# Local-window attention with an FFN: the values of a pair of heads as one TensorE block, and the order drawn up anew

## The chip, the cores and the metric

One core of a Trainium2 chip. The metric is the device time of one execution in microseconds (us). Engines: TensorE (PE) for matmuls, with its weight loads (PEld) beside them; VectorE (DVE); ScalarE (ACT); GpSimd (POOL); SyncE (SP), which issues the DMAs.

## The reference, cut to what is computed

```python
# q_l,k_l,v_l: (8, 8, 512, 64); q_g,k_g,v_g: (8, 8, 32, 64)
k_all, v_all = concat([k_g, k_l], 2), concat([v_g, v_l], 2)
out_g = softmax(q_g @ k_all.T / 8) @ v_all                  # 32 global rows see everything
s_ll  = where(abs(i - j) <= 32, q_l @ k_l.T / 8, -1e9)      # local rows: a window, and the global keys
out_l = softmax(concat([q_l @ k_g.T / 8, s_ll])) @ concat([v_g, v_l])
x = concat([out_g, out_l], 2) -> (8 * 544, 512)             # 8 heads x 64
h = x @ w_in                                                # 512 -> 2048, weights in float64
return (h * erf(softplus(h))) @ w_out                       # 2048 -> 512
```

## The kernel before

**The work.** There are 64 heads (8 batches of 8). `attention(b, h, key)` records the steps of one head. For a pair of heads one TensorE block of 64x32 tiles makes the scores of both (tiles `s`, 32 blocks). For each head DVE adds the mask and takes the maximum, ACT takes the exponentials (tile `sm`; for the first `BIASED` heads with the maximum as a bias, after them with a subtraction on DVE or POOL), PE transposes them in full 128x128 shape (`t`), ACT or DVE copies the result to SBUF (`pt`, two buffers), and PE makes the values `o` in 128x32 tiles: a block of 16 small products for each head, 64 blocks in all. DVE normalizes them into `xn`. For every four heads `attention_global(b, j, ...)` does the same for the 32 global rows: scores `ga`, `gb` (64x32 tiles), transposes `gt`, values `go` (128x32 tiles), 16 blocks of each.

The FFN runs as full 128x128 products of 512 columns, a high and a low part of each factor (three matmuls for one product): `h` (`unit`), the gate (`gate`: softplus and erf on ACT, tiles `sp`, `gh`, `gl`), `op` (`project`). A first pass takes three eighths of the hidden columns, batch by batch, between the attention heads; a second pass takes the rest when attention is done, with the products `pa` to `pd` of a seven-product scheme for pairs of batches. Weights come as float64 and are turned into float32 parts on DVE and ACT (`to_fp32`, `keep_in`, `keep_unit`; tiles `top_in`, `top_out`, `top_l_in`, `top_k_out`).

**What sets the order.** Nothing runs when `attention` or `gate` is called: each step is recorded by `Program.add(ways, key, fn, reads, writes, ...)`, where `ways` names the engines that may do it with an assumed time for each, and `key` is its due time. `Program.schedule()` (line 159) plays the steps through once, on the host, with these times. For each engine it takes the ready step of lowest key whose buffers are free and writes the order out; that order, engine by engine, is the program's. `crowded` (line 190) keeps the number of PE instructions within a stretch of time under a limit (`CROWD`, `STRETCH`, `EVADE`); `PORT` charges DVE for working beside POOL; `SHARED` (line 40) names the range of keys in which a step may go to POOL as well as DVE; `fill` puts spare matmuls into PE's idle time at the start. Keys come from the constants at the top (`HKEYS` for the heads, `GOFF`, `POFF`, `GATE1`, `PROJ1` and others for the FFN). PSUM has two banks with tag `h` and six with tag `a`; scores, transposes, values and `op` share the six.

Of the kernel before, what the change touches and what calls it, by code (L numbers as in the profile page):

```python
# [21 lines left out]
P = 128  # L22
# [7 lines left out]
CROWD, STRETCH, EVADE = 254, 4.013, 0.27  # L30
# [3 lines left out]
HKEYS = ((0, -5.063), (10, -3.503), (22, 0.608), (64, 30.894))  # L34
STEP, GKEY = 0.023, -0.868
QLEAD, VLEAD, RLEAD, XLEAD = 0.459, 0.046, 0.011, 2.412
# [4 lines left out]
TPAIR = 2.626  # L41
KEEP, KSTEP, FIRST = 16.147, 2.595, (-2.849, 0.951)
CVO = (50.84, 53.645, 53.996, 48.864, 55.397)
QLEAD2, XDEL, SLOTS = 10.999, 1.259, 11
GATE1, GATE2, PROJ1, PROJ2 = (3.909, 9.618, 11.922), (13.773, 23.579, 27.539), 17.617, 26.859
SPT = 0.35
BIAS, AHEAD = 1.072, 15.956
# [3 lines left out]
SLACK, PORT = {"PE": 0.8, "SP": 0.8}, 0.7  # L51
# [7 lines left out]
WLEAD = 0.011  # L59
LATER, GFIRST = 8, (-2.568, -2.486)  # L60
NORMAL = 1.125 * 2.0**-15
STRAIGHT, XLATE = True, -0.932
# [44 lines left out]
class Program:  # L107
# [9 lines left out]
    def add(self, ways, key, fn, reads=(), writes=(), moved=0.0, heat=0, ins=None):  # L117
# [9 lines left out]
        op.heat, op.ins = heat, ins or heat // 256  # L127
# [24 lines left out]
        self.ops.append(op)  # L152
        return op
# [5 lines left out]
    def schedule(self):  # L159
# [28 lines left out]
        warmth, issued = [], []  # L188

        def crowded(n):  # L190

            t = 0.0
            for at, m in reversed(issued):
                n += m
                if at <= now - STRETCH:
                    break
                if n > CROWD:
                    t = max(t, at + STRETCH - now)
                    break
            return t  # L200

        def fill():
            dur = fill_dur if now > COLD else 2 * fill_dur
            until["PE"] = max(since, now) + dur
            heapq.heappush(events, (until["PE"], -1, 0, None))
            if now >= since:
                op = Op()
                op.eng, op.ways, op.fn, op.key, op.start, op.heat = "PE", {"PE": dur}, fill_fn, 0.0, now, fill_heat
                op.new, op.bufs = [], []
                order.append(op)  # L210
                warmth.append((now, fill_heat))

# [6 lines left out]
        while events or any(o.eng is None for o in self.ops) and ahead < 1e3:  # L219
# [14 lines left out]
            while picked:  # L234
                picked = False
                for e, q in ready.items():
# [4 lines left out]
                    while until[e] <= now and (dense or q and q[0][0] <= line[front].key + ahead):  # L241
# [4 lines left out]
                        item = dense.pop(0) if dense_only and dense else heapq.heappop(q)  # L246
# [6 lines left out]
                        if any(free[k] < n for k, n in need.items()) or elsewhere(op, e):  # L253
                            skipped.append(item)
                            continue
# [50 lines left out]
def kernel(  # L306
# [109 lines left out]
    def attention(b, h, key):  # L416
# [17 lines left out]
        if h % 2 == 0:  # L434
# [39 lines left out]
        if biased:  # L474
            add({"ACT": 1.05}, key, exps, [TAB, MX], [SM])
# [16 lines left out]
        PT = abuf([P, 4, P], f"pt_{nm}", "pt", 2)  # L492
        add({"PE": 0.5}, key + STEP * 2, transposes, [SM, CS], [T, PT], heat=512, ins=8)
# [3 lines left out]
        def values():  # L497
# [9 lines left out]

        add({"PE": 0.64}, key + STEP * 3, values, [PT, VA, VB], [O], heat=1040, ins=64)
        RS = abuf([P, 4, 1], f"rs_{nm}", "rs", 2)
        add({"DVE": 0.07},  # L510
            key + STEP * 3,
            lambda: dve.tensor_scalar(RS.ap, O.ap[:, :, D : D + 1], 1e-9, None, op0=ALU.add),
            [O],
            [RS],
        )
        add({"DVE": 0.09}, key + STEP * 3, lambda: dve.reciprocal(RS.ap, RS.ap), [], [RS])

        def norm(e):
            if e == "DVE":
                dve.tensor_tensor(  # L520
                    XN.ap[:, :, r0 : r0 + D], O.ap[:, :, :D], RS.ap.to_broadcast([P, 4, D]), ALU.mult
                )
            else:
                for t in range(4):
                    act(XN.ap[:, t, r0 : r0 + D], O.ap[:, t, :D], AF.Copy, scale=RS.ap[:, t, :])

        add({"DVE": 0.34, "ACT": 0.85}, key + STEP * 3, norm, [O, RS], [XN])
# [20 lines left out]
        if h % 4 == 3:  # L548
            more = b, h // 4, [st["va", i] for i in range(4)], [st["qk", i] for i in range(2)]
            if b == 0 and LATER:  # L550
                held.append((*more, GFIRST[h // 4]))
            else:
                attention_global(*more, key + GKEY)
# [4 lines left out]
    held, GTURN, X0 = [], fixed(None), {}  # L558
# [33 lines left out]
    def attention_global(b, j, VA, qk, key):  # L592
        nm = f"{b}_{j}"
# [19 lines left out]
        add({"PE": 1.15}, key, scores, [*qk[0], *qk[1]], [GA, GB, GTURN], heat=1088, ins=32)  # L613
        M, NM = abuf([P, 2], f"gm_{nm}", "gm", 2), abuf([P, 1], f"gn_{nm}", "gn", 2)
        add({"DVE": 0.57}, key, lambda: dve.tensor_reduce(M.ap[:, 0:1], GA.ap, axis=AX.X, op=ALU.max), [GA], [M])
# [44 lines left out]
        add({"PE": 0.88}, key + STEP * 3, values, [GT, *VA], [O], heat=1560, ins=96)  # L660
# [44 lines left out]
    def to_fp32(key, src, name, TOP, ABS, deps, lead=RLEAD):  # L705
# [21 lines left out]
        add({"DVE": 1.75}, key, bits, [RAW], [TOP.buf])  # L727
# [12 lines left out]
    class View:  # L740
# [3 lines left out]
        def ap(self):  # L744
            return self.f(self.buf.ap)
# [58 lines left out]
    def keep_in(q, key):  # L804
# [9 lines left out]
        def part_of(m, a, k):  # L814
            A, ap = a
            O = mbuf([P, 2, 2, P], F32R, f"part_{q}_{m}", "os", 4)
            add({"ACT": 0.36, "DVE": 0.25}, k, lambda e: copy(e, O.ap[:, 0], ap()), [A.buf], [O])
            add(
                {"POOL": 0.88, "DVE": 0.4},
# [14 lines left out]
        def sum_of(out, a, b, op, k):  # L834
            add(
                {"DVE": 0.4, "POOL": 0.8},
# [19 lines left out]
    def load_x(ps, c, key):  # L856
# [5 lines left out]
        for i in range(2):  # L862
# [23 lines left out]
            add({"DVE": 0.0014 * n, "ACT": 0.0022 * n + 0.1}, k, split_hi, [RAW], [HI])  # L886
            add({"POOL": 0.0048 * n + 0.3, "DVE": 0.0026 * n + 0.15}, k, split_lo, [RAW, HI], [LO])
# [39 lines left out]
    def gate(ps, c, us, key, after=(), turn=(), line=()):  # L927
# [3 lines left out]
        def erf():  # L931
# [10 lines left out]
            {"ACT": 2.57 + 1.29 * (ps == 0) + 1.09 * len(us)},  # L942
# [6 lines left out]
        for n, ((v, Hb, more), SPb) in enumerate(zip(us, SP)):  # L949
# [5 lines left out]
                {"DVE": 0.75, "POOL": 1.5},  # L955
# [5 lines left out]
            add({"DVE": 0.43, "ACT": 0.55}, k, lambda e, SPb=SPb, GH=GH: copy(e, GH.ap, SPb.ap), [SPb, *after], [GH, *turn])  # L961
            add(
                {"DVE": 0.75, "POOL": 1.5},
# [16 lines left out]
    def project(ps, c, G, at, order, after=None):  # L980
# [15 lines left out]
        for t in range(nt):  # L996
            for n, rows in enumerate(order):
                need = [x for g, _, v in rows for x in (*G[g], *W["out", ps, v // 2])]
                add(
                    {"PE": 0.685 * len(rows)},  # L1000
# [82 lines left out]
    def pair_blocks(pr, key):  # L1083
# [11 lines left out]
        def block(name, n, A, k):  # L1095
# [17 lines left out]
            add({"DVE": 0.95, "ACT": 1.1}, k, hi, [A, ATTN], [HI])  # L1113
            add({"POOL": 2.8, "DVE": 1.55}, k, lo, [A, HI, ATTN], [LO])
            blocks[name] = (HI, LO)

        def sum_of(out, a, b, op, k):
            add(
                {"DVE": 1.2, "POOL": 2.5},
# [20 lines left out]
    def products(name, q, X, key):  # L1140
# [17 lines left out]
        def product(n, m, x, start, k):  # L1158
            add({"PE": 1.37}, k, lambda: mm(n, m, x, start), [M[m], *X[x]], [bank[n]], heat=3072)
# [63 lines left out]
    def last_unit(q, X, key):  # L1223
# [17 lines left out]
        for r in range(2):  # L1241
            add({"PE": 1.43}, key + 0.01 * r, lambda r=r: mm(r), [*M.values(), *(t for b in X.values() for t in b)], [HP], heat=3072)
# [127 lines left out]
```

## Time and profile before

| | |
|---|---|
| time of the runs | 920.95 us median of 3 (920.82 to 922.83) |
| the profiled execution's span | 920.8 us, 22337 instructions |
| busy: PE, PEld | 897.3 us (97%), 720.7 us (78%) |
| busy: DVE, ACT, POOL | 667.2 us (72%), 570.1 us (62%), 61.7 us (7%) |
| chain of work that ended last | PE 84%, DMA 6%, DVE 6%, issue 2%, ACT 1% |
| DMA over the span | 188.23 MB, mean 204 GB/s |

An engine's busy time is the union of its instructions. Matmuls are pipelined, so their listed durations overlap; what one costs is read from the distance of starts. A number in brackets behind a row is the idle time of the engine just before it, with what ended it; "issue" means that the engine waited for nothing that the profile shows.

### The profile page before, as it was taken

How to read it: one execution, taken by the hardware profiler on the slowest of the kernel's cores; microseconds unless marked ns; L12 is line 12 of the kernel's file. 1: busy time of each engine (PE TensorE's matmuls, PEld its weight loads, DVE VectorE, ACT ScalarE, POOL GpSimd, SP SyncE). 2: the span in 40 equal slices, each digit the busy share in tenths (PEclk: the TensorE clock that was granted, in tenths of full speed). 3: DMA queues.
4: the chain of work that ended last, by engine and by line, in shares of the span. 5: the costliest groups of instructions: out<-in, count | busy, mean ns of one | idle time of the engine just before them, and what ended most of it. 6: DMA issues, size and time to landing. Idle time of an engine off the chain costs nothing.

```text
span 920.8 us, 22337 instructions
## 1 busy us (share of the span) xinstructions
PE 897.3 (97%) x8814; PEld 720.7 (78%) x8814; DVE 667.2 (72%) x1733; ACT 570.1 (62%) x975; POOL 61.7 (7%) x51
## 2 busy tenths in 40 slices
PE   8799989999999999999999999999999999999998
PEld 5576767777777778888888888888888888888886
DVE  4698989978979897768857867648674677445562
ACT  4578986656757676866855569425862476335760
POOL 0003543131100000000000000000000000000000
PEclk9899999999999999999999999999999999999999
DMA  9698986979697885823458953644355535455121
GB/s 338 224 305 265 317 270 214 301 240 285 213 313 252 274 281 177 293 110 124 151 204 299 343 181 124 217 139 154 89 183 173 193 91 159 126 170 167 66 80 68
DMA packets 110017, 188.23 MB, mean 204 GB/s; under 512 B 15576, under 2 KB 39384, under 8 KB 109912
## 3 DMA queue, kind: packets, MB, share of 16 engines
q1 hardware_dynamic: 109912, 186.79, 61.8%
q8 instruction: 70, 1.15, 0.5%
q14 instruction: 35, 0.29, 0.1%
HBM read 145.59 MB, written 41.16 MB: 203 GB/s over the span
## 4 chain that ended last, share of the span: by engine, by line
PE 84%; DMA 6%; DVE 6%; issue 2%; ACT 1%; SPq 1%; DVEq 0%; ACTq 0%
PE op L344 38%; PE h L344 12%; PE pd L344 6%; PE pc L344 6%; PE pa L344 6%; PE pb L344 3%; PE o L344 3%; PE t L345 3%; PE s L344 2%; DMA wq<-part 2%; PE h_g L344 2%; DMA vb<-in_vB_dram 1%; DMA xsc<-xT 1%; DMA k<-in_kE_dram 1%; PE gt L345 1%
## 5 line engine op out<-in xcount | busy, mean ns | idle before, releaser
L344 PE MATMUL op<-wouth,gh 128*128 128x512 f32 x544 | 215.9, 397 | 0.4 <-DVE mx L356 0.4
L344 PE MATMUL op<-wouth,gl 128*128 128x512 f32 x544 | 212.1, 390 | 0.2 <-issue 0.2
L344 PE MATMUL op<-woutl,gh 128*128 128x512 f32 x544 | 212.0, 390 | 0.0
L347 ACT ACT_TABLE_LOAD x108 | 138.6, 1283 | 2.7 <-PEq L1357 0.7
L344 PEld LDWEIGHTS op<-wouth,gh 128*128 128x128 f32 x544 | 102.2, 188 | 23.2 <-issue 2.0
L344 PEld LDWEIGHTS op<-wouth,gl 128*128 128x128 f32 x544 | 102.1, 188 | 21.8
L344 PEld LDWEIGHTS op<-woutl,gh 128*128 128x128 f32 x544 | 102.2, 188 | 19.6
L356 DVE TENSOR_TENSOR gl<-sp,gh 128x512 fp32r<-128x512 f32 x129 | 89.4, 707 | 27.8 <-ACT gh L346 18.3
L346 ACT ACTIVATE gh<-sp 128x512 fp32r<-128x512 f32 x94 | 57.2, 627 | 83.8 <-PE op L344 71.1
L344 PE MATMUL h<-xh,winh 128*128 128x512 f32 (+1 forms) x216 | 85.8, 397 | 0.3 <-ACT hs L346 0.3
L344 PE MATMUL h<-xh,winl 128*128 128x512 f32 (+1 forms) x216 | 82.5, 382 | 0.0
L344 PE MATMUL h<-xl,winh 128*128 128x512 f32 (+1 forms) x216 | 82.5, 382 | 0.0
L346 ACT ACTIVATE sp<-sp 128x512 f32<-128x512 f32 x136 | 75.9, 621 | 0.5
L356 DVE CUSTOM_DVE_ANT_0 sm<-s,cs 128x128 f32<-128x128 f32 x256 | 57.1, 283 | 12.2 <-DMA cs<-in_cst_dram 7.0
L344 PE MATMUL pa<-xh_B,wq 128*128 128x512 f32 x160 | 55.8, 389 | 0.0
L344 PE MATMUL pd<-xh_T,wq 128*128 128x512 f32 x160 | 55.6, 389 | 0.0
L346 ACT ACTIVATE hs<-h 128x512 f32<-128x512 f32 x44 | 26.0, 595 | 41.5 <-PE h L344 41.3
L344 PEld LDWEIGHTS h<-xh,winh 128*128 128x128 f32 x216 | 41.1, 190 | 9.3 <-issue 1.0
L356 DVE TENSOR_TENSOR pair<-u,pc 128x512 f32<-128x512 f32 x40 | 27.4, 684 | 27.6 <-PE pc L344 27.5
L344 PEld LDWEIGHTS h<-xh,winl 128*128 128x128 f32 x216 | 41.0, 190 | 8.0
L344 PEld LDWEIGHTS o<-va,pt 128*32 128x32 f32 x768 | 31.7, 109 | 19.1 <-issue 11.2
L344 PEld LDWEIGHTS h<-xl,winh 128*128 128x128 f32 x216 | 41.1, 190 | 6.7
(163 smaller groups left out, 1687.0 us busy)
## 6 DMA issues: line engine op xcount, KB each, us to landing
wq<-wq SPq DMA_DIRECT2D x140, 256.0 KB, 3.3
vb<-in_vB_dram SPq DMA_DIRECT2D x64, 325.0 KB, 5.2
rx<-xsc SPq DMA_DIRECT2D x30, 512.0 KB, 5.4
va<-in_vA_dram SPq DMA_DIRECT2D x64, 195.0 KB, 4.8
k<-in_kE_dram SPq DMA_DIRECT2D x32, 384.0 KB, 5.1
wq<-part SPq DMA_DIRECT2D x35, 256.0 KB, 4.3
q<-in_qT_dram SPq DMA_DIRECT2D x32, 272.0 KB, 4.9
part<-os SPq DMA_DIRECT2D x34, 256.0 KB, 3.4
```

Source lines behind the costliest of these rows:

```text
L344: pe = lambda n, *a, **k: pinned(nc.tensor.matmul(n, *a, **k))
L345: tr = lambda *a, **k: pinned(nc.tensor.transpose(*a, **k))
L346: act = lambda *a, **k: pinned(nc.scalar.activation(*a, **k))
L347: table = lambda name: pinned(nc.scalar.preload_act_table_set(name))
L356: return lambda *a, **k: pinned(f(*a, **k))
```

## The change

It does five things.

1. From head 16 on (`PAIRED`), the values of the two heads of a pair are one recorded step (`pair`), which waits for the `pt` of both heads. Their normalizations (`normalize`, the same operations as before) follow it. In batches 6 and 7 the values of the global rows are in the same step as the pair of heads 2, 3 or 6, 7 (`GOJOIN`), and the global scores in the same step as that pair's scores (`GSJOIN`, `joint`).
2. The planner gives each PE step a mode (`S` for scores, `O` for values, `F` for full products and transposes) and adds a time from `TURN` where the mode changes. While PE is in mode S or O, a ready step of the same mode counts as `NEAR` = 10.893 keys earlier.
3. `PORT` goes from 0.7 to 1.0, with the charge limited to 1.6 us in place of 1.5 times the step's own time; many assumed times are reset. `SHARED` ends at key 0.191 instead of 17.961, so that steps with later keys go to DVE alone.
4. `pt` and `sm` have four buffers each instead of two. `crowded` uses a longer stretch (5.5) between 8 and 36 us, and `EVADE` goes from 0.27 to 0.515.
5. All keys are drawn up anew, and `BIASED` is 28 instead of 30.

```diff
-CROWD, STRETCH, EVADE = 254, 4.013, 0.27
+CROWD, STRETCH, EVADE = 254, 4.013, 0.515
+LOADED = (8.0, 36.0, 5.5)
-HKEYS = ((0, -5.063), (10, -3.503), (22, 0.608), (64, 30.894))
+HKEYS = ((0, -4.186), (11, -1.133), (22, 2.638), (64, 28.435))
-GOFF, POFF = 1.452, 1.865
-WIN, WOUT = (-2.963, -1.41, -1.202), (3.958, 3.604, 3.417)
-BIASED, AG = 30, 3
-SHARED = (-99.0, 17.961)
+GOFF, POFF = 6.702, 2.351
+WIN, WOUT = (-1.182, -0.883, -2.317), (6.11, 7.043, 6.921)
+BIASED, AG = 28, 3
+SHARED = (-99.0, 0.191)
-KEEP, KSTEP, FIRST = 16.147, 2.595, (-2.849, 0.951)
+KEEP, KSTEP, FIRST = 17.877, 2.241, (18.664, 20.991)
-GATE1, GATE2, PROJ1, PROJ2 = (3.909, 9.618, 11.922), (13.773, 23.579, 27.539), 17.617, 26.859
+GATE1, GATE2, PROJ1, PROJ2 = (20.257, 19.313, 15.951), (15.777, 23.93, 18.604), 21.217, 28.842
-SLACK, PORT = {"PE": 0.8, "SP": 0.8}, 0.7
+SLACK, PORT = {"PE": 0.8, "SP": 0.8}, 1.0
+TURN = {"FS": 0.11, "FO": 0.11, "SF": 0.35, "OF": 0.28, "SO": 0.31, "OS": 0.30}
+NEAR = 10.893
+PAIRED, GOJOIN, GSJOIN, PTS = 16, 6, 6, 4
+SMS, SPARED = 4, 0
-LATER, GFIRST = 8, (-2.568, -2.486)
+LATER, GFIRST = 9, (-3.478, -13.073)
...
+            stretch = LOADED[2] if LOADED[0] <= now < LOADED[1] else STRETCH
...
-                        item = dense.pop(0) if dense_only and dense else heapq.heappop(q)
+                        if dense_only and dense:
+                            item = dense.pop(0)
+                        elif e == "PE" and mode != "F" and NEAR:
+                            item = min(q, key=lambda i: (i[0] - (NEAR if i[2].mode == mode else 0.0), i[1]))
+                            q.remove(item)
+                            heapq.heapify(q)
+                        else:
+                            item = heapq.heappop(q)
...
+                        if e == "PE":
+                            dur += TURN.get(mode + op.mode, 0.0)
+                            mode = op.mode
                         if e == "DVE" and op.port:
-                            dur += PORT * min(max(0.0, until["POOL"] - now), 1.5 * dur)
+                            dur += PORT * min(max(0.0, until["POOL"] - now), 1.6)
...
-            add({"PE": 1.24}, key, scores, [Q, K], SS, heat=2048, ins=128)
+            if h % 4 == 2 and b >= GSJOIN:
+                GA, GB, more = global_scores(b, h // 4, [st["qk", 0], (Q, K)])
+                G0[b, h // 4] = GA, GB
+
+                def joint():
+                    scores()
+                    more()
+
+                add({"PE": 1.9}, key, joint, [*st["qk", 0], Q, K], [*SS, GA, GB, GTURN], heat=3136, ins=160, mode="S")
+            else:
+                add({"PE": 1.02}, key, scores, [Q, K], SS, heat=2048, ins=128, mode="S")
...
-        SM = abuf([P, 4, P], f"sm_{nm}", "s", 2)
+        SM = abuf([P, 4, P], f"sm_{nm}", "s", SMS)
...
-        PT = abuf([P, 4, P], f"pt_{nm}", "pt", 2)
+        PT = abuf([P, 4, P], f"pt_{nm}", "pt", PTS)
...
-        add({"PE": 0.64}, key + STEP * 3, values, [PT, VA, VB], [O], heat=1040, ins=64)
+        if h % 4 == 3 and b >= GOJOIN:
+            joined = global_probs(*group, key + GKEY)
+        if NH * b + h - h % 2 < PAIRED:
+            add({"PE": 0.55}, key + STEP * 3, values, [PT, VA, VB], [O], heat=1040, ins=64, mode="O")
+            normalize(O, XN, r0, nm, key)
+        elif h % 2 == 0:
+            st["o"] = values, [PT, VA, VB], O, r0, nm
+        else:
+            first, need, O0, *rest = st["o"]
+            last, more, GO = joined or (None, [], None)
+
+            def pair():
+                first()
+                values()
+                if last:
+                    last()
+
+            add({"PE": 1.11 + 0.72 * (GO is not None)},
+                key + STEP * 3,
+                pair,
+                [*need, PT, VA, VB, *more],
+                [O0, O] + [GO] * (GO is not None),
+                heat=2080,
+                ins=128 + 96 * (GO is not None),
+                mode="O",
+            )
+            normalize(O0, XN, *rest, key)
+            normalize(O, XN, r0, nm, key)
+            if joined:
+                global_rows(*group[:2], GO, key + GKEY)
```

`global_scores`, `global_probs` and `global_rows` are the three parts of `attention_global`, their operations unchanged.

## Rows read from the trace of the kernel before

**Rows 1.** Stages: us; busy PE, PEld, DVE, ACT, POOL (instructions); clock; DMA; GB/s.

```profile
58.00:160.00 102.00, 93.65 (x1780) 71.35 (x1781) 93.93 (x332) 85.65 (x185) 39.54 (x29) 0.98 0.83 268
160.00:364.00 204.00, 201.01 (x3329) 155.15 (x3328) 179.09 (x631) 132.35 (x237) 18.68 (x15) 1.00 0.82 263
364.00:920.80 556.80, 553.26 (x2531) 461.62 (x2529) 356.74 (x594) 319.79 (x470) 0.00 (x0) 1.00 0.49 162
```

**Rows 2.** Timeline of PE: start, us, instruction; one head's values among full products.

```profile
207.47 0.39 PE L344 MATMUL h<-xh,winl 128*128 128x512 f32 x1
207.79 0.24 PE L344 MATMUL o<-va,pt 128*32 128x65 f32 x1
...
208.38 0.55 PE L345 MATMUL gt<-cs,pg 128*128 128x128 f32 x3
```

**Rows 3.** Timeline of PE: values of two heads side by side.

```profile
215.42 0.24 PE L344 MATMUL o<-va,pt 128*32 128x65 f32 x1
...
216.47 0.50 PE L344 MATMUL h<-xh,winh 128*128 128x512 f32 x1
216.81 0.39 PE L344 MATMUL h<-xl,winh 128*128 128x512 f32 x1
```

**Rows 4.** Timeline of PE: global scores alone, a pair's scores alone, both together.

```profile
199.70 1.01 PE L344 MATMUL ga<-k,q 64*32 64x480 f32 x8
...
200.75 0.44 PE L345 MATMUL t<-cs,sm 128*128 128x128 f32 x2
...
203.16 1.16 PE L344 MATMUL s<-k,q 64*32 64x128 f32 x64
204.25 0.24 PE L344 MATMUL o<-va,pt 128*32 128x65 f32 x1
...
219.41 1.16 PE L344 MATMUL s<-k,q 64*32 64x128 f32 x64
...
221.43 0.50 PE L344 MATMUL op<-wouth,gh 128*128 128x512 f32 x1
```

**Rows 5.** Timeline of PE: first and last stretch of values, of scores.

```profile
12.67 0.24 PE L344 MATMUL o<-va,pt 128*32 128x65 f32 x1
...
360.74 0.24 PE L344 MATMUL o<-va,pt 128*32 128x65 f32 x1
...
5.37 0.45 PE L344 MATMUL s<-k,q 64*32 64x128 f32 x16
...
344.31 1.01 PE L344 MATMUL ga<-k,q 64*32 64x480 f32 x8
```

**Rows 6.** Timeline of DVE, POOL, PE near 128 us; chain that ended last (two pieces).

```profile
127.34 3.37 DVE L356 SCALAR_TENSOR_TENSOR top_out<-raw_out,top_out 128x512 int32<-128x512 int32 x2
127.19 2.97 POOL L356 TENSOR_TENSOR sp<-sp,hs 128x512 f32<-128x512 f32 x2 [4.47 <-ACT sp L346]
132.97 0.41 PE L344 MATMUL gx<-cs,xg 128*128 128x64 f32 x2 [3.42 <-DVE xg L356]
...
133.82 4.34 PE h L344 x12
374.56 5.44 PE h L344 x24
```

**Rows 7.** DVE groups (busy us, mean ns; idle) from 40, last from 364; stage 40:364.

```profile
L356 DVE SCALAR_TENSOR_TENSOR top_out<-raw_out,top_out 128x512 int32<-128x512 int32 x12 | 13.0, 1080 | 0.4
L356 DVE SCALAR_TENSOR_TENSOR top_k_out<-raw_k_out,top_k_out 128x512 int32<-128x512 int32 x12 | 8.3, 693 | 0.4
L356 DVE TENSOR_TENSOR gl<-sp,gh 128x512 fp32r<-128x512 f32 x106 | 71.2, 688 | 25.6 <-ACT gh L346 16.4 <-PE op L344 7.4
...
40.00:364.00 324.00, 312.15 (x5543) 237.97 (x5542) 290.55 (x1030) 229.95 (x450) 60.77 (x46) 0.99 0.83 266
```

**Rows 8.** Waits of PE: waiter, releaser, us, times, longest; 0:58, then 58:364.

```profile
PE o L344 <- issue: 4.7, 2, 3.5
...
PE t L345 <- issue: 0.7, 1, 0.7
```

More of the change, by code (lines that the diff above doesn't have):

```diff
@@ L115, in __init__, with add @@
         self.psum = psum
-    def add(self, ways, key, fn, reads=(), writes=(), moved=0.0, heat=0, ins=None):
+    def add(self, ways, key, fn, reads=(), writes=(), moved=0.0, heat=0, ins=None, mode="F"):
         if "DVE" in ways and not SHARED[0] <= key < SHARED[1]:
@@ L187, in schedule @@
         fill_dur, fill_fn, fill_heat, since, before = self.idle
-        warmth, issued = [], []
+        warmth, issued, mode = [], [], "F"
         def crowded(n):
             t = 0.0
+            stretch = LOADED[2] if LOADED[0] <= now < LOADED[1] else STRETCH
             for at, m in reversed(issued):
                 n += m
-                if at <= now - STRETCH:
+                if at <= now - stretch:
                     break
                 if n > CROWD:
-                    t = max(t, at + STRETCH - now)
+                    t = max(t, at + stretch - now)
                     break
@@ L202, in fill @@
         def fill():
+            nonlocal mode
             dur = fill_dur if now > COLD else 2 * fill_dur
@@ L211, in fill @@
                 warmth.append((now, fill_heat))
+                mode = "F"
         taken = []
@@ L252, in schedule @@
                             need[b.pool, b.tag] = need.get((b.pool, b.tag), 0) + 1
-                        if any(free[k] < n for k, n in need.items()) or elsewhere(op, e):
+                        spared = SPARED if op.mode == "S" else 0
+                        if any(free[k] < n + spared for k, n in need.items()) or elsewhere(op, e):
                             skipped.append(item)
@@ L474, in attention @@
         if biased:
-            add({"ACT": 1.05}, key, exps, [TAB, MX], [SM])
+            add({"ACT": 1.18}, key, exps, [TAB, MX], [SM])
         else:
@@ L506, in values @@
                 )
-        add({"PE": 0.64}, key + STEP * 3, values, [PT, VA, VB], [O], heat=1040, ins=64)
[L509 to L527, printed above, removed]
+        group = b, h // 4, [st["va", i] for i in range(h % 4 + 1)], [st["qk", i] for i in range(h % 4 // 2 + 1)]
+        joined = None
+        if h % 4 == 3 and b >= GOJOIN:
[26 more added lines that the diff above has]
+                global_rows(*group[:2], GO, key + GKEY)
         if h % 2 == 1:
@@ L547, in attention @@
                 add({"SP": 4 * SPT}, key + STEP * 4, store, [XT, ATTN], [XSC[b, p]], moved=262.0)
-        if h % 4 == 3:
-            more = b, h // 4, [st["va", i] for i in range(4)], [st["qk", i] for i in range(2)]
+        if h % 4 == 3 and not joined:
             if b == 0 and LATER:
-                held.append((*more, GFIRST[h // 4]))
+                held.append((*group, GFIRST[h // 4]))
             else:
-                attention_global(*more, key + GKEY)
+                attention_global(*group, key + GKEY)
         if NH * b + h == LATER:
@@ L556, in attention, with normalize, norm @@
                 attention_global(*more)
-    held, GTURN, X0 = [], fixed(None), {}
+    def normalize(O, XN, r0, nm, key):
+        RS = abuf([P, 4, 1], f"rs_{nm}", "rs", 2)
+        add({"DVE": 0.07},
+            key + STEP * 3,
+            lambda: dve.tensor_scalar(RS.ap, O.ap[:, :, D : D + 1], 1e-9, None, op0=ALU.add),
+            [O],
+            [RS],
+        )
+        add({"DVE": 0.09}, key + STEP * 3, lambda: dve.reciprocal(RS.ap, RS.ap), [], [RS])
+        def norm(e):
+            if e == "DVE":
+                dve.tensor_tensor(
+                    XN.ap[:, :, r0 : r0 + D], O.ap[:, :, :D], RS.ap.to_broadcast([P, 4, D]), ALU.mult
+                )
+            else:
+                for t in range(4):
+                    act(XN.ap[:, t, r0 : r0 + D], O.ap[:, t, :D], AF.Copy, scale=RS.ap[:, t, :])
+        add({"DVE": 0.34, "ACT": 0.85}, key + STEP * 3, norm, [O, RS], [XN])
+    held, GTURN, X0, G0 = [], fixed(None), {}, {}
     def straight(p, XN, key):
@@ L592, in attention_global, with global_scores @@
     def attention_global(b, j, VA, qk, key):
+        values, need, O = global_probs(b, j, VA, qk, key)
+        add({"PE": 0.72}, key + STEP * 3, values, need, [O], heat=1560, ins=96, mode="O")
+        global_rows(b, j, O, key)
+    def global_scores(b, j, qk):
         nm = f"{b}_{j}"
@@ L611, in scores, with global_probs @@
                 )
-        add({"PE": 1.15}, key, scores, [*qk[0], *qk[1]], [GA, GB, GTURN], heat=1088, ins=32)
+        return GA, GB, scores
+    def global_probs(b, j, VA, qk, key):
+        nm = f"{b}_{j}"
+        if (b, j) in G0:
+            GA, GB = G0.pop((b, j))
+        else:
+            GA, GB, scores = global_scores(b, j, qk)
+            add({"PE": 0.9}, key, scores, [*qk[0], *qk[1]], [GA, GB, GTURN], heat=1088, ins=32, mode="S")
         M, NM = abuf([P, 2], f"gm_{nm}", "gm", 2), abuf([P, 1], f"gn_{nm}", "gn", 2)
-        add({"DVE": 0.57}, key, lambda: dve.tensor_reduce(M.ap[:, 0:1], GA.ap, axis=AX.X, op=ALU.max), [GA], [M])
+        add({"DVE": 0.56}, key, lambda: dve.tensor_reduce(M.ap[:, 0:1], GA.ap, axis=AX.X, op=ALU.max), [GA], [M])
         add({"DVE": 0.13}, key, lambda: dve.tensor_reduce(M.ap[:, 1:2], GB.ap, axis=AX.X, op=ALU.max), [GB], [M])
@@ L658, in values, with global_rows @@
                     )
-        add({"PE": 0.88}, key + STEP * 3, values, [GT, *VA], [O], heat=1560, ins=96)
+        return values, [GT, *VA], O
+    def global_rows(b, j, O, key):
+        nm = f"{b}_{j}"
         RS = abuf([P, 1], f"gr_{nm}", "gr", 2)
@@ L725, in normal @@
             dve.scalar_tensor_tensor(a, ABS.ap().bitcast(F32), NORMAL, a, op0=ALU.is_gt, op1=ALU.mult)
-        add({"DVE": 1.75}, key, bits, [RAW], [TOP.buf])
+        add({"DVE": 1.8}, key, bits, [RAW], [TOP.buf])
         add({"DVE": 0.6}, key, normal, [ABS.buf], [TOP.buf])
@@ L816, in part_of @@
             O = mbuf([P, 2, 2, P], F32R, f"part_{q}_{m}", "os", 4)
-            add({"ACT": 0.36, "DVE": 0.25}, k, lambda e: copy(e, O.ap[:, 0], ap()), [A.buf], [O])
+            add({"ACT": 0.34, "DVE": 0.22}, k, lambda e: copy(e, O.ap[:, 0], ap()), [A.buf], [O])
             add(
-                {"POOL": 0.88, "DVE": 0.4},
+                {"POOL": 0.88, "DVE": 0.34},
                 k,
@@ L835, in sum_of @@
             add(
-                {"DVE": 0.4, "POOL": 0.8},
+                {"DVE": 0.34, "POOL": 0.8},
                 k,
@@ L954, in gate @@
             add(
-                {"DVE": 0.75, "POOL": 1.5},
+                {"DVE": 0.62, "POOL": 1.5},
                 k,
@@ L960, in gate @@
             )
-            add({"DVE": 0.43, "ACT": 0.55}, k, lambda e, SPb=SPb, GH=GH: copy(e, GH.ap, SPb.ap), [SPb, *after], [GH, *turn])
+            add({"DVE": 0.36, "ACT": 0.54}, k, lambda e, SPb=SPb, GH=GH: copy(e, GH.ap, SPb.ap), [SPb, *after], [GH, *turn])
             add(
-                {"DVE": 0.75, "POOL": 1.5},
+                {"DVE": 0.62, "POOL": 1.5},
                 k,
@@ L999, in project @@
                 add(
-                    {"PE": 0.685 * len(rows)},
+                    {"PE": 0.681 * len(rows)},
                     at(n) + 0.01 * t + (TPAIR * (t // 2) if ps == 0 else 0.0),
@@ L1111, in lo @@
                     )
-            add({"DVE": 0.95, "ACT": 1.1}, k, hi, [A, ATTN], [HI])
-            add({"POOL": 2.8, "DVE": 1.55}, k, lo, [A, HI, ATTN], [LO])
+            add({"DVE": 0.72, "ACT": 1.08}, k, hi, [A, ATTN], [HI])
+            add({"POOL": 2.8, "DVE": 1.23}, k, lo, [A, HI, ATTN], [LO])
             blocks[name] = (HI, LO)
@@ L1118, in sum_of @@
             add(
-                {"DVE": 1.2, "POOL": 2.5},
+                {"DVE": 1.15, "POOL": 2.5},
                 k,
@@ L1241, in last_unit @@
         for r in range(2):
-            add({"PE": 1.43}, key + 0.01 * r, lambda r=r: mm(r), [*M.values(), *(t for b in X.values() for t in b)], [HP], heat=3072)
+            add({"PE": 1.44}, key + 0.01 * r, lambda r=r: mm(r), [*M.values(), *(t for b in X.values() for t in b)], [HP], heat=3072)
         Hb = mbuf([P, SL], F32, f"hs_g{q}", "hs", 6)
```

28 lines of the change are left out of this document (14 added, 14 removed).

## The prediction

> **What bounds the kernel now.** I read the stages first [rows 1]. From 364 us to the end TensorE (PE) is busy 553.26 of 556.80 us, and the rest of that stretch is the last addition and store: it runs matmuls of one shape back to back, and nothing in a new order can shorten it. The attention heads, with first-pass FFN blocks between them, lie before 364 us. From 160 to 364 PE is busy 201.01 of 204 us, from 58 to 160 only 93.65 of 102. VectorE (DVE) is busy 93.93 and 179.09 us there, 92% and 88%. So PE is the bound, and time can come from two places alone: useless time inside PE's busy time, and PE's waits, most of them before 160 us.
>
> The useless time is in the changes of shape, read from starts of neighbouring matmuls. A stretch of one head's values among FFN matmuls goes 207.47, 207.79, 208.38 [rows 2]: the first values start 0.32 us after the last FFN matmul, where FFN matmuls follow each other every 5.44/24 = 0.227 us [rows 6], and the block holds 0.59 us. Where two heads happen to stand together they take 215.42 to 216.47 = 1.05 us [rows 3], so the second adds 0.46, and the first FFN matmul behind them takes 216.81 - 216.47 = 0.34. One visit to the values' shape thus costs 0.09 (in) + 0.13 (0.59 - 0.46) + 0.11 (out) = 0.33 us beyond its matmuls. Scores act alike: a pair's scores alone 1.09 us, global scores alone 1.05, both together 219.41 to 221.43 = 2.02 [rows 4], so 0.12 is saved inside; with the same 0.2 for in and out a visit costs 0.32. There are 62 separate stretches of values and 44 of scores (the first and last of each are in [rows 5]), 34.5 us in all.
>
> The waits: the longest between 58 and 160 us is 3.42 us at 132.97, on a DVE result [rows 6]. DVE was late because two SCALAR_TENSOR_TENSOR took 3.37 us from 127.34, beside GpSimd (POOL) work of 2.97 us from 127.19; such an instruction takes 0.693 us alone [rows 7], so two take 1.39. The stop was paid twice: the twelve FFN matmuls behind it took 4.34 us instead of 5.44/2 = 2.72 [rows 6]; it is where most of the stretch's clock loss lies (granted 0.98 of full speed, 1.00 in the next) [rows 1].
>
> **The change, part by part.**
>
> Values in pairs, global values joined. Before: 64 value blocks and 16 global ones fall into 62 stretches. After: heads 0 to 15 stay single (PAIRED), 48 heads make 24 pairs, 4 of the 16 global blocks (batches 6 and 7) ride with a pair: 16 + 24 + 12 = 52 blocks, even if no two meet. NEAR makes the planner prefer a ready block of the shape PE is in, by up to 10.9 keys. Without it 80 blocks met so that 18 stretches were saved; with it I let 52 become 43. Bounds 52 and 36. So 19 visits go (10 to 26): 19 x 0.33 = 6.3 us (3.3 to 8.6).
>
> Scores. 32 + 16 blocks in 44 stretches; 4 joins make 44 blocks, but one global block of the last batches already mixes with a pair's scores in one stretch (the row at 344.31 in [rows 5]). With NEAR I take 37 stretches (44 to 30): 7 x 0.32 = 2.2 us (0 to 4.5). Together 8.5 us (3.3 to 13.1), all on the path, since PE has no gaps to absorb it.
>
> GpSimd. SHARED ends at key 0.19 instead of 17.96, so nearly all 46 POOL operations from 40 to 364 us, 60.77 us [rows 7], go to DVE. A 128x512 two-input operation on DVE with POOL silent takes 0.688 us [rows 7]: 46 x 0.683 (the sm and x forms are a shade shorter) = 31.4 us more. In return DVE is no longer held up. The raw top_out form has a mean of 1.080 us over 12, the same form for top_k_out 0.693 [rows 7]: 12 x 0.387 = 4.6 us. The same subtraction, form by form, gives 20.7 us over 29 instructions in the whole trace (13.1 of it from 58 to 160 us). DVE thus gains 10.7 us of work, none on PE, and loses its irregular stops. Of PE's time I book the stop at 132.97: 3.48 (1.16 us of scores from 128.39, then nothing until 132.97) plus 4.34 - 2.72 = 1.6, together 5.1 us (0 if another DVE delay stands in its place).
>
> The Trainium skill bears on this (SBUF — State Buffer, section "SBUF: two separate sides"): the port pair of VectorE and GpSimd is an exclusive lock, whoever starts first keeps it for the whole instruction, and the other is fully blocked. The trace agrees: 3.37 us for two instructions that take 1.39, beside 2.97 us of POOL [rows 6, 7]. Were every DVE instruction blocked in that way, all 60.77 us of POOL would come back to DVE, its load would fall by 29 us, and with no new waits the sum would be 907.4; the page itself limits the lock to DVE instructions with two SBUF inputs or in a two-port mode. The sum goes by the 20.7 us of the rows.
>
> New waits. From 58 to 160 us DVE was busy 93.93 us and had 29 POOL operations beside it [rows 1]: 93.93 + 29 x 0.683 - 13.1 = 100.6 us in a stretch of 102. Copies with a choice can go to ScalarE (busy 85.65 of 102), and later FFN work hides lateness. A pair's block also waits for both heads' probabilities; PE's queue is in order, so FFN matmuls, transposes and the next scores queue behind it, and the first head's normalization on DVE is later by one head. Four copies of the probabilities and exponentials (PTS, SMS) against two are the cover; without them each pair would wait for the DVE of one head. Bounds: 0, and the stretch at DVE's present share of 0.921: 100.6/0.921 = 109.2, so +7.2 us. I take +2.5, nearer the low end, because in rows 1 the next stretch runs PE without gaps at 88% of DVE.
>
> Start. Before 58 us PE waited 4.7 us in two pieces for its own instructions at the values, 3.5 the longest [rows 8]. The new account (LOADED, EVADE, first keys) spaces blocks there, but the same instructions must come in. I take 0, bounds -3.5 to +3.5. FFN keys (GATE, PROJ, FIRST) after 364 us: 0, because PE there always has the next product; without that cover a late gate shows as a PE gap, which rows 1 do not have.
>
> Sum, against the profiled 920.8 us: -8.5 - 5.1 + 2.5 = -11.1, so 909.7; the runs' median 920.95 lies 0.15 above the span: **909.9 us**.
>
> **Rivals.**
> (a) DVE bounds 58 to 160 us: the full +7.2 instead of +2.5, 914.6. For: 100.6 of 102 us. Against: ScalarE has 16 us free there.
> (b) It does not do what it says: the shape visits hardly fall, because two heads already stood together (13 of the 47 stretches from 80 us on), and no block of another pair is ready in time. Low ends 3.3 and 0: 920.95 - 3.3 - 5.1 + 2.5 = 915.1.
> (c) Slower: DVE bounds all of 58 to 364 us and PE runs out of FFN rows. DVE then has 93.93 + 179.09 + 44 x 0.683 - 19.8 = 283.3 us; at its present share, 273.0/306 = 0.892, the stretch is 317.6 us, and the time 920.95 + 11.6 = 932.6. It is slower than before from a share below 283.3/306 = 0.926. For: share and PE shortening pull against each other. Against: attention may end later at no cost as long as first-pass FFN blocks remain, and at 374.56 they still run [rows 6].
> (d) Slower: pairs outrun the instruction supply. The shorter of the two stops at the values was 4.7 - 3.5 = 1.2 us [rows 8]. If all 24 pairs met one, 24 x 1.2 = 28.8, so 938.7; it eats the gain from ten pairs on. Against: from 58 us on, where two heads stood together 13 times, the largest instruction waits at PE are 0.7 us once [rows 8].
>
> **How the numbers follow.** Forecast 0.60 (902 to 915 by its terms), (a) 0.14, (b) 0.08, (c) 0.12, (d) 0.06. About 0.2%, 1.8 us, is what a measurement here can tell from no change. Of the forecast's own 0.60, 0.01 falls within it, of (a) and (b) 0.02, of (c) 0.03, of (d) 0.01; 0.01 of (c) lies on the fast side. Faster 0.59 + 0.20 + 0.01 = 0.80; same 0.07; slower 0.08 + 0.05 = 0.13. The range for 8 in 10 runs from 902 (turns at their high end and half of the start's bound) to 921 (where (c) and (d) begin): some 0.06 lie below and 0.14 above.
>
> **What would show it.** The values' stretches number 36 to 52, with blocks of some 1.05 us, and 1.7 to 1.8 us where global values ride along; scores 30 to 44. Attention ends some 8 to 12 us earlier than 361 us, or as late with fewer FFN blocks left behind it. POOL is all but empty; the raw top_out form falls to 0.69 us; no PE gap of 3 us beside a doubled DVE instruction. DVE is above 92% from 58 to 160 us, and ScalarE fuller. After attention PE stays full. The prediction is wrong if PE gaps between 40 and 364 us sum to more than the 11.85 us of now [rows 7], if instruction waits stand before pair blocks, or if the stretches stay above 55.

## The result, and the profile after

The changed kernel takes 910.52 us (median of 4 runs, 908.43 to 911.66) against 921.89 us before in the same comparison: ratio 0.9872, 95% interval 0.9845 to 0.9898. A later comparison gave 0.988 (0.9853 to 0.9907). The profiled execution took 910.62 us with a span of 908.5, so some 2.1 us lie around the span. The prediction booked 0.15, because it held the span of one execution against the median of others; in the runs of the kernel before whose span is on record, some 1.8 us lie around it.

The page of the changed kernel, its busy times and the granted clock in 40 slices:

```profile
span 908.5 us, 22227 instructions
PE 885.5 (97%) x8797; PEld 719.1 (79%) x8804; DVE 681.2 (75%) x1811; ACT 548.5 (60%) x928; POOL 6.0 (1%) x9
PEclk9999999999999999999999999999999999999999
```

Its stages (us; busy PE, PEld, DVE, ACT, POOL; clock; DMA share; GB/s), to be held against [rows 1]:

```profile
0.00:58.00 58.00, 50.46 (x1223) 34.48 (x1230) 49.42 (x221) 40.81 (x112) 6.05 (x9) 1.00 0.87 307
58.00:160.00 102.00, 97.78 (x1794) 76.44 (x1796) 94.18 (x339) 80.18 (x160) 0.00 (x0) 1.00 0.84 275
160.00:364.00 204.00, 196.35 (x3323) 156.84 (x3312) 178.36 (x646) 128.82 (x220) 0.00 (x0) 0.99 0.80 255
364.00:908.50 544.50, 540.91 (x2476) 451.33 (x2475) 359.23 (x608) 298.69 (x437) 0.00 (x0) 1.00 0.51 166
```

After 364 us PE is full as before, but the rest is 12.3 us shorter: attention ends at nearly the same time (358.9 us against 361.9) with more FFN matmuls done. From 58 to 160 PE's gaps fell from 8.35 to 4.22 us; from 160 to 364 they rose from 2.99 to 7.65. The visits to the small shapes fell further than forecast: 37 stretches of values instead of 62, 32 of scores instead of 44 (counted in the trace). One pair of heads among FFN products, and the first FFN product of all (timeline of PE):

```profile
116.26 0.39 PE L365 MATMUL h<-xh,winl 128*128 128x512 f32 x1
116.58 0.24 PE L365 MATMUL o<-va,pt 128*32 128x65 f32 x1
...
117.62 0.49 PE L365 MATMUL h<-xh,winh 128*128 128x512 f32 x1
117.95 0.40 PE L365 MATMUL h<-xl,winh 128*128 128x512 f32 x1
...
38.97 0.48 PE L365 MATMUL h<-xh,winh 128*128 128x512 f32 x1
```

The pair's block holds 1.04 us, as the neighbouring heads of [rows 3] did. The FFN begins at 38.97 us; before it began at 58.28.

PE's waits from 58 to 364 us (who waited for whom: us, times, longest), against [rows 6, 8]:

```profile
PE s L365 <- DMA k<-in_kE_dram: 2.6, 1, 2.6
PE gb L365 <- issue: 1.8, 1, 1.8
PE go L365 <- DVE os L377: 1.6, 1, 1.6
PE t L366 <- issue: 1.3, 1, 1.3
PE t L366 <- DVE mx L377: 1.2, 2, 1.0
```

The stop of 3.42 us beside a doubled DVE instruction is gone, and four new ones of 1.3 to 2.6 us stand elsewhere. The longest, before a pair's scores, was paid twice:

```profile
206.21 1.95 PE L365 MATMUL s<-k,q 64*32 64x128 f32 x64 [2.63 <-DMA k<-in_kE_dram]
208.08 0.79 PE L365 MATMUL h<-xh,winh 128*128 128x512 f32 x1
208.68 0.63 PE L365 MATMUL h<-xl,winh 128*128 128x512 f32 x1
209.10 0.63 PE L365 MATMUL h<-xh,winl 128*128 128x512 f32 x1
```

Behind it the scores take 1.95 us (1.16 usually) and FFN matmuls follow each other at up to 0.42 us (208.68 to 209.10) instead of 0.23: PE ran on at the lower of its two clock levels for some 3.3 us (granted 0.96 of full speed from 200 to 240 us, 1.00 in the 40 us on either side).

**A ledger of both traces.** For each block on PE the time to the start of the next block is held against its usual time in this place. What is over, with the spare matmuls before 58 us, comes in all to 38.7 us before and 40.2 us after:

| us over | before | after |
|---|---|---|
| spare matmuls (54; 44, of which the trace has 37) | 15.2 | 11.4 |
| 0 to 58 us, other | 9.6 | 8.9 |
| 58 to 160 us | 10.7 | 7.3 |
| 160 us to the end of attention | 3.2 | 12.6 |

By this account the waits grew by 1.5 us in sum, and by difference the 37 visits fewer gave 12.3 + 1.5 = 13.8 us, 0.37 each. The figure is no better than the usual times it rests on: where these are fitted to all traces of this case instead, the visits give 10 to 13 us (an estimate), and the waits do not grow. The pages agree that PE's waits hardly moved in sum: it is idle for 920.8 - 897.3 = 23.5 us before, for 23.0 after, and for 24.0 in a repeat of the changed kernel (`after_again`) whose trace has all records. The time went out of PE's busy time.

### The profile page after: what moved, and what is told of

It is laid out like the page before. It is cut to its first block, busy times and chain, and to the rows that moved or that the text cites. A ratio compares the mean times of both kernels' runs of the same rounds, so it can differ in the third digit from the quotient of the medians.

```text
span 908.5 us, 22227 instructions
## 1 busy us (share of the span) xinstructions
PE 885.5 (97%) x8797; PEld 719.1 (79%) x8804; DVE 681.2 (75%) x1811; ACT 548.5 (60%) x928; POOL 6.0 (1%) x9
## 4 chain that ended last, share of the span: by engine, by line
PE 61%; DVE 2%; DMA 1%; ACT 0%; issue 0%; DVEq 0%; ACTq 0%
PE op L365 33%; PE pd L365 6%; PE pc L365 6%; PE pa L365 6%; PE h L365 6%; PE pb L365 3%; PE h_g L365 2%; DVE sm L377 1%; DMA wq<-part 1%; DMA out_dram<-os 0%; DVE gl L377 0%; DVE sp L377 0%; DVE part L377 0%; DVE gm L377 0%; DVE xT L377 0%
## 5 line engine op out<-in xcount | busy, mean ns | idle before, releaser
L367 ACT ACTIVATE gh<-sp 128x512 fp32r<-128x512 f32 x74 | 46.0, 630 | 118.2 <-PE op L365 105.1
L377 DVE CAST gh<-sp 128x512 fp32r<-128x512 f32 x62 | 26.1, 421 | 46.7 <-PE op L365 46.7
L377 DVE TENSOR_TENSOR os<-op,os 128x512 f32<-128x512 f32 (+1 forms) x35 | 23.5, 675 | 31.9 <-PE op L365 28.3
```

The lines of the kernel that those rows point to most:

```text
L367: act = lambda *a, **k: pinned(nc.scalar.activation(*a, **k))
L377: return lambda *a, **k: pinned(f(*a, **k))
```

## The experiments

**The theory:** the time went with PE's changes of shape, about 0.33 us for each visit. **The rival:** it went with the doubled DVE instructions beside GpSimd (GpSimd's lock, 3.37 us instead of 1.39 in [rows 6, 7]) and the better start; a change of shape is hidden because matmuls overlap.

### The price of a visit, with order and work kept

A full-shape matmul whose result is overwritten at once stands in front of each pair's values and each pair's scores (`dummy_front`), then between the two heads' values (`dummy_values_mid`), then also in the middle of the scores (`dummy_both_mid`).

```diff
             def pair():
+                dummy()   # dummy_front: pe(O.ap[:, 0, :D], ident, sel, start=True, stop=True)
                 first()
+                dummy()   # the other two: here instead
                 values()
...
             for t in range(4):
+                if t == 0: pe(SS[0].ap[:, 3, :D], ident, sel, start=True, stop=True)   # dummy_both_mid: t == 2
```

> Changed kernel, same order; each of the 32 score blocks and each of the 24 pair blocks begins with one full-shape 128x128 by 64-column matmul that is overwritten at once. It stands outside the small-tile stretch, so no visit is added. Such a matmul (gx) holds PE about 0.14 us: both theories expect 56 x 0.14 = 7.8 us above the changed kernel (910.5), about 918; it is the baseline for the next two.

> As dummy_front, but in the 24 pair blocks the full-shape matmul stands between the values of the two heads. Work and order are the same; 24 visits to the values' shape are added. Theory (time went with the changes of shape, 0.33 us each): 24 x 0.33 = 7.9 us above dummy_front, 6 to 9.5. Rival (the gain came from the lock of GpSimd and the better start; changes of shape are hidden in pipelining): under 2 us above it.

> As dummy_values_mid, and in the 32 score blocks the full-shape matmul stands in the middle instead of in front: 32 more visits to the scores' shape. Theory: 32 x 0.32 = 10.2 us above dummy_values_mid, 7 to 13. Rival: under 2 us above it.

Measured, beside a kernel before of 922.64 us: 915.73 (ratio 0.9922, 0.9901 to 0.9944; 5.2 us over the changed kernel's 910.52, 4.6 in ratio, where both theories had 7.8), 918.62 (0.9953, 0.9935 to 0.9971), 922.68 (1.0004, 0.9989 to 1.002). Timeline of PE, one pair's values in the first kernel, then in the second:

```profile
118.38 0.39 PE L365 MATMUL h<-xh,winl 128*128 128x512 f32 x1
118.61 0.33 PE L365 MATMUL o<-cs 128*128 128x64 f32 x2
...
119.91 0.50 PE L365 MATMUL h<-xh,winh 128*128 128x512 f32 x1
120.25 0.40 PE L365 MATMUL h<-xl,winh 128*128 128x512 f32 x1
```

```profile
119.84 0.39 PE L365 MATMUL h<-xh,winl 128*128 128x512 f32 x1
...
120.75 0.43 PE L365 MATMUL o<-cs 128*128 128x64 f32 x2
...
121.70 0.50 PE L365 MATMUL h<-xh,winh 128*128 128x512 f32 x1
122.04 0.40 PE L365 MATMUL h<-xl,winh 128*128 128x512 f32 x1
```

From the last FFN matmul to the second one behind, it is 120.25 - 118.38 = 1.87 us with the odd matmul in front and 122.04 - 119.84 = 2.20 in the middle: the visit costs 0.33 us, to the hundredth what [rows 2, 3] gave. Four of the five such places from 60 us on show it; at the fifth a wait is in between in both kernels. The odd matmul itself holds PE 1.87 - 1.69 = 0.18 us (1.69 is 117.95 - 116.26 in the changed kernel's pair shown above). Scores in the first and the third kernel:

```profile
141.96 0.39 PE L365 MATMUL op<-wouth,gl 128*128 128x512 f32 x1
...
143.87 0.40 PE L365 MATMUL op<-woutl,gh 128*128 128x512 f32 x1
```

```profile
147.67 0.40 PE L365 MATMUL op<-wouth,gl 128*128 128x512 f32 x1
...
149.89 0.40 PE L365 MATMUL op<-woutl,gh 128*128 128x512 f32 x1
```

1.91 against 2.22 us: 0.31. The rival's claim that a visit is hidden falls. Yet the end moved less than the sum. The stretches of values rose from 41 to 61 in the traces (not by 24, because the odd matmul in front already splits some neighbours): 20 x 0.33 = 6.6 us, measured 2.9. Scores, 35 to 64: 29 x 0.31 = 9.0 us, measured 4.1 (the profiled spans moved by 6.8, but the profiled execution of the third kernel is the slowest of its 12). The first kernel is no pure baseline either: its odd matmuls add 4 visits of values and 3 of scores, so that some 56 x 0.18 + 7 x 0.33 = 12.4 us on the spot moved the end by 4.6 to 5.2. The theory's ranges were missed on the low side both times, the rival's 2 us on the high side. At these prices (2.9/20 and 4.1/29, 0.14 us each) the 37 visits would be worth some 5 us of the 11.4 at the end (an estimate). So a visit is shown to cost time; that the visits carry all of the gain is not shown. The stretch from 58 to 380 us of the three kernels shows where it went:

```profile
58.00:380.00 322.00, 313.37 (x5292) 259.56 (x5281) 285.16 (x1007) 218.85 (x394) 0.00 (x0) 1.00 0.81 260
```

```profile
58.00:380.00 322.00, 317.85 (x5307) 257.18 (x5297) 283.07 (x1006) 215.40 (x390) 0.00 (x0) 0.99 0.81 255
```

```profile
58.00:380.00 322.00, 318.92 (x5324) 250.26 (x5324) 279.80 (x1006) 212.05 (x389) 0.00 (x0) 0.99 0.79 250
```

PE's gaps are 8.63, 4.15 and 3.08 us. With 20 more visits 4.5 us of waiting vanished: a PE that comes later finds more of its operands there. For the scores' visits, 1.1 us vanished, and what took up the rest of the difference is open.

### Pairs, joins and preference taken out, order planned again

```diff
-PAIRED, GOJOIN, GSJOIN, PTS = 16, 6, 6, 4
+PAIRED, GOJOIN, GSJOIN, PTS = 64, 9, 9, 4      # singles, singles_no_preference
-NEAR = 10.893
+NEAR = 0                                       # no_preference, singles_no_preference
```

> Changed kernel without pairs and joins (values of every head a block of its own, global rows apart); preference for the same shape and everything else kept, order planned again: 52 stretches of values and 38 of scores instead of 37 and 32. Theory (0.33 and 0.32 us for each): 15 x 0.33 + 6 x 0.32 = 6.9 us above the changed kernel, 917.4; 914 to 921 with other waits. Rival (GpSimd and start): within 2 us of 910.5.

> Changed kernel with the preference for the same shape set to 0, pairs and joins kept: 41 stretches of values, 40 of scores. Theory: 4 x 0.33 + 8 x 0.32 = 3.9 us above the changed kernel, 914.4; 911.5 to 918. Rival: within 2 us of 910.5.

> Changed kernel with neither pairs and joins nor the preference; GpSimd still almost empty, new keys kept: 59 stretches of values, 44 of scores, nearly the 62 and 44 of before. Theory: 22 x 0.33 + 12 x 0.32 = 11.1 us above the changed kernel, 921.6, as slow as before; 917 to 926. Rival: the gain stays, 910 to 913.

Beside a kernel before of 922.7 us: `singles` 921.49 (ratio 0.9986, 0.9963 to 1.0009), `no_preference` 925.23 (1.002, 0.9993 to 1.0047), `singles_no_preference` 924.29 (1.0021, 0.9996 to 1.0046). Each loses all or nearly all of the gain, which speaks against the rival: GpSimd is as empty as in the changed kernel (busy 3.6 to 6.3 us), and the FFN begins nearly as early (40 to 46 us, 39 there). The theory has the last in its range (917 to 926), the first just above it (914 to 921), and misses `no_preference` by 7 us (911.5 to 918). Visits alone don't rank them: with 81 stretches `no_preference` is no faster than the one with 103. The same ledger gives it 13.3 us from 58 to 160 us and 14.2 behind, against 7.3 and 12.6 in the changed kernel, and 15.2 of spare matmuls. From 58 to 380 us its PE waits 8.7 us for its own instructions ("issue", the longest 3.6), against 3.6 in the changed kernel. The keys fit one set of blocks; a new plan with the same keys brings waits of its own.

### The blocks alone, with the keys of before

The constants of before at the top of the kernel (keys, GpSimd's range, `PORT`, no `TURN`), with pairs, joins, four buffers and the preference. The assumed times written into the steps stay those of the changed kernel, so this is not quite the plan of before with new blocks.

```diff
-HKEYS = ((0, -4.186), (11, -1.133), (22, 2.638), (64, 28.435))
+HKEYS = ((0, -5.063), (10, -3.503), (22, 0.608), (64, 30.894))
-SHARED = (-99.0, 0.191)
+SHARED = (-99.0, 17.961)
...
-TURN = {"FS": 0.11, "FO": 0.11, "SF": 0.35, "OF": 0.28, "SO": 0.31, "OS": 0.30}
+TURN = {}
```

> The keys, assumed times and GpSimd share of before, with pairs, joins, four buffers and the preference: 45 stretches of values, 29 of scores, GpSimd as busy as before. Theory (shape visits carry the gain, keys and GpSimd add little): 17 x 0.33 + 15 x 0.32 = 10.4 us under before (921.9), 911.5; 908 to 916. Rival (GpSimd's lock and the start): no faster than 919.

922.58 us, ratio 0.9997 (0.9978 to 1.0016). The theory's second half falls: with 45 and 29 stretches, 32 fewer than before (some 10.4 us at the local price), nothing is gained; the theory had 908 to 916. The ledger: spare matmuls 19.2 us (73 of them), 17.3 us from 58 to 160, 5.7 behind, 12.6 us more waste in all than before. "No faster than 919" is what the rival expected, with GpSimd as busy and the FFN as late (58.88 us) as before; but the three kernels above lose the gain with neither. Fewer visits are worth their price only in an order that keeps PE supplied. That order is the other half of this change.

### GpSimd alone, order kept

```diff
+        # after_pool_back: TO_POOL names 37 operations that GpSimd had before; their place in the changed order is kept
+        if op.eng == "DVE" and hasattr(op, "whole") and "POOL" in op.whole[0] and "+".join(sorted(b.name for b in op.bufs)) in TO_POOL:
+            op.whole[1]("POOL")
+            continue
         op.fn(*([op.eng] if len(op.ways) > 1 else []))
...
-        op.fn(*([op.eng] if len(op.ways) > 1 else []))
+        # before_pool_to_dve, in the kernel before
+        eng = "DVE" if op.eng == "POOL" and "DVE" in op.ways and op.key > 0.191 else op.eng
+        op.fn(*([eng] if len(op.ways) > 1 else []))
```

> Changed kernel, its order kept, but 37 operations that the kernel before gave to GpSimd (59 us by its assumed times) go back to GpSimd in their places. DVE loses 37 x 0.683 = 25 us of work and is held up again for some 20 us. Theory (taking GpSimd out moves little in sum, but single stops of some us come with it): 0 to 5 us above the changed kernel, 910.5 to 915.5. Rival (the lock carries the gain): 8 us or more above, over 918.5.

> Kernel before, its order kept, but all GpSimd operations of key over 0.19 run on DVE in their places: DVE has some 26 us more work and 20 us fewer stops. Theory: the 5.1 us stop at 133 us goes, up to as much comes back in places where DVE is full: 917 to 922 against 921.9. Rival (the lock carries the gain): 914 or less.

`after_pool_back`: 915.38 us, ratio 0.991 (0.9894 to 0.9927), 0.003 to 0.004 above the changed kernel, some 3 us, as the theory had it. `before_pool_to_dve`: 922.5 us, 1.0005 (0.9986 to 1.0024), no change; the theory had 917 to 922, the rival 914 or less. In its trace the lock is gone and the stop is not (timeline of DVE, then of PE, against [rows 6]):

```profile
128.20 1.42 DVE L356 SCALAR_TENSOR_TENSOR top_out<-raw_out,top_out 128x512 int32<-128x512 int32 x2
132.49 0.66 PE L344 MATMUL gx<-cs,xg 128*128 128x64 f32 x2 [2.13 <-DVE xg L356]
```

Two instructions take 1.42 instead of 3.37 us, but PE still waits 2.13 us: DVE gets to them 0.86 us later than before, and an operation that GpSimd had (0.69 us at 131.13) now stands between them and the result that PE waits for.

In `after_pool_back` the lock is back, and a stop with it (timeline of DVE, POOL, PE):

```profile
117.64 1.57 DVE L418 TENSOR_SCALAR top_out<-raw_out 128x512 int32<-128x512 int32 x1
119.25 3.36 DVE L418 SCALAR_TENSOR_TENSOR top_out<-raw_out,top_out 128x512 int32<-128x512 int32 x2
117.63 6.11 POOL L418 TENSOR_TENSOR sp<-sp,hs 128x512 f32<-128x512 f32 x4
125.45 0.47 PE L406 MATMUL op<-wouth,gh 128*128 128x512 f32 x1 [2.40 <-DVE xn L418]
...
126.52 0.63 PE L406 MATMUL op<-wouth,gh 128*128 128x512 f32 x1
126.94 0.63 PE L406 MATMUL op<-woutl,gh 128*128 128x512 f32 x1
```

The same place in the changed kernel:

```profile
116.62 1.42 DVE L377 SCALAR_TENSOR_TENSOR top_out<-raw_out,top_out 128x512 int32<-128x512 int32 x2
121.05 0.47 PE L365 MATMUL op<-wouth,gh 128*128 128x512 f32 x1 [0.43 <-DVE xn L377]
```

The two doubled instructions take 3.36 us beside GpSimd and 1.42 without it, and PE waits 2.40 us for a later DVE result instead of 0.43. The wait is paid twice, as in [rows 6]: the granted clock is 0.61 from 125 to 129 us, and the matmuls come 0.42 us apart. Together that is some 3.6 us, about what the end lost. Other waits differ too, so it is likely, not shown, that this stop alone makes the difference.

### Eighty DVE instructions fewer, order kept

Without the addition of 1e-9 to the softmax sums, which changes nothing in float32; the reciprocal reads PSUM directly.

```diff
-            lambda: dve.tensor_scalar(RS.ap, O.ap[:, :, D : D + 1], 1e-9, None, op0=ALU.add),
+            lambda: None,
-        add({"DVE": 0.09}, key + STEP * 3, lambda: dve.reciprocal(RS.ap, RS.ap), [], [RS])
+        add({"DVE": 0.09}, key + STEP * 3, lambda: dve.reciprocal(RS.ap, O.ap[:, :, D : D + 1]), [], [RS])
...
-            dve.tensor_scalar(RS.ap, O.ap[:, D : D + 1], 1e-9, None, op0=ALU.add)
-            dve.reciprocal(RS.ap, RS.ap)
+            dve.reciprocal(RS.ap, O.ap[:, D : D + 1])
```

> The changed kernel unaltered, beside the next two: 909 to 912, ratio 0.987 to before. No theory differs on it.

> Changed kernel, order kept, without the addition of 1e-9 to the sums of the softmax (the sum is at least 1, in float32 it changes nothing): 64 TENSOR_SCALAR of 0.15 us on DVE and 16 for the global rows, 10 us of DVE, none of PE. Theory (with fewer changes of shape the new order leaves PE waiting for DVE, which is why inserted visits cost only half their local price): 3 to 6 us faster than the changed kernel, 905 to 908. Rival (PE alone is the bound, the halves came from chance): less than 1.5 us faster.

> Kernel before, order kept, without the addition of 1e-9: the same 10 us of DVE less. Theory (in the old order PE, slowed by 106 visits, waits less for DVE, above all after 160 us): 0 to 3 us faster than before, less than the changed kernel gains. Rival (DVE was as much a bound before as after): as much as the changed kernel gains.

Beside a kernel before of 924.13 us: `after_again` 912.43 (0.988), `after_less_dve` 910.37 (0.9851, 0.9825 to 0.9876), `before_less_dve` 920.53 (0.9969, 0.9953 to 0.9985). The 80 instructions have listed durations of 12 us in sum, but they overlap with their neighbours: DVE's busy time fell by 5.2 us in the new order (681.4 to 676.2) and by 7.9 in the old one (667.2 to 659.3), not by 10. The old order gains 3 us in ratio, the new one 2.7 (its interval overlaps that of the unaltered kernel). So PE waits for DVE now and then in both, by about the same; the theory (3 to 6 us in the new order, less in the old) is not borne out. `after_less_dve` has the lowest ratio of all kernels here; that it beats the changed kernel is likely, not shown.

## Why the prediction was right, point by point

**The total** was right (909.9 predicted, 910.52 measured) and lay in the range. That it came so close is luck: by the ledger the visits gave 13.8 us instead of 8.5 and the start 4.5 instead of nothing, while the stop and the new waits took 6.0 where 2.6 was to be won. Of the 11.4 us the experiments account for some 5 by the visits (at the price of the inserted ones at the end, an estimate) and some 3 by the emptier GpSimd; the rest lies in the order and the start, and no run takes these apart.

**The price of a visit** was right as PE pays it on the spot: 0.33 and 0.32 us from starts in the trace, 0.33 and 0.31 where only the place of one matmul was changed. That all of it is on the path, "since PE has no gaps to absorb it", was wrong: of the inserted visits less than half reached the end (2.9 of 6.6 us, 4.1 of 9.0), for the values because PE's gaps shrank.

**The number of visits** was mis-sized: 37 and 32 instead of 43 and 37. The term is 25 x 0.33 + 12 x 0.32 = 12.1 us instead of 8.5, inside its bounds. The step that failed was the guess that 52 blocks of values meet in 43 stretches: they met in 37. NEAR has the smaller part in it: with NEAR at 0 (`no_preference`) there are 41, so that 11 of the 15 come from how the new plan falls. For scores it counts for more: 40 without it, 32 with it.

**GpSimd** was wrong in its mechanism. The lock on DVE was read rightly (3.37 us against 1.39, and 1.42 without GpSimd), but 5.1 us for the stop at 132.97 was too much: in the order of before, taking GpSimd out gives nothing, and the stop keeps 2.13 us. That is the low bound of the term. In the new order GpSimd's return costs some 3 us. DVE's load rose as its stops fell, which the prediction had in its sum (31.4 against 20.7 us) and did not carry to this stop.

**New waits** had the right sign, the wrong place and too small a size. They were booked from 58 to 160 us, where DVE would be full, at 2.5 us. There the loss fell, from 10.7 to 7.3 us; from 160 us on, where 88% of DVE was read as harmless, it rose from 3.2 to 12.6. Of the three longest there, two are for late DVE results (1.6 us in front of global values behind a pair, 1.0 for maxima), as the prediction had it in kind; the longest, 2.6 us, is for the transfer of a pair's keys, which it had not thought of. Taken with the stop of GpSimd's term, -5.1 + 2.5 = -2.6 was booked from 58 us on, and +6.0 came.

**The start** was booked at 0 and gave 4.5 us (15.2 + 9.6 against 11.4 + 8.9), slightly over its bound of 3.5: the FFN begins 19 us earlier. Which of the new keys does it was not tried alone.

**The rivals.** (a) did not come: from 58 to 160 us PE's share rose. (b) did not: visits fell far. (c) did not, though 283 us of DVE was right in kind: DVE is busy 94.18 + 178.36 = 272.5 us from 58 to 364, since 12 us of its work moved ahead of 58 us (49.42 us there, 37.44 before). (d) came three times instead of 24: waits for instructions of 1.8, 1.3 and 0.5 us beside global scores, transposes and values. Their length was in kind right, the frequency as its "against" had it.

**The signs.** One sign of being wrong came: PE's gaps from 40 to 364 us sum to 13.19 us, more than the 11.85 of before, and in a repeat (`after_again`) to 14.24. The prediction's own test thus says wrong, though the total says right: the gaps before 160 us fell and those behind it rose by more. Waits for instructions did not stand before pair blocks (one of 0.5 us stands inside one, among its global values). ScalarE was to be fuller from 58 to 160 us; it was busy 80.18 us there instead of 85.65. The rest came as described: stretches, lengths of blocks (1.04 us, and 1.73 with global values), an empty GpSimd, the raw `top_out` form at 0.69 us, DVE at 92.3% from 58 to 160 us, PE full after attention.

## What to carry to other kernels

Read the price of a change of shape from starts of neighbouring matmuls, and count the visits: here the trace gave 0.33 us, and an odd matmul moved by a few places confirmed it. Such a saving reaches the end only where PE then finds work: a part of it comes back as waits for other engines, and in an order planned for other blocks all of it. What a lock that doubles an instruction costs hangs on the order too: nothing was won where the work that took the lock then stood in the same queue, and some 3 us were lost where PE waited for what came behind the doubled instructions.

## What was not expected of the hardware

A wait of 2.63 us at PE was followed by some 3.3 us at the lower of its two clock levels (1.2 and 2.4 GHz) (matmuls of 512 columns every 0.42 us instead of 0.23), so that the stop cost about 4 us in all; the one of 3.42 us in [rows 6] acted alike. Waits of 1.3 and 1.8 us were not followed by it in the changed kernel, whose granted clock is 1.00 from 58 to 160 us. The length of the wait alone doesn't decide it: in `after_again` PE waited 2.18 us at the same place, before a pair's scores, and the clock stayed at 1.00 (209 to 212 us), while the 2.13 us in `before_pool_to_dve` were followed by 0.54 (133 to 136 us).
